# Windowed attention with sinks and a routed block: scores and band masks in 64x64 tiles, casts on GpSimd, weights by the hardware queue

## The chip, the cores and the metric

The kernel runs on one core of a Trainium2 chip. The metric is the device time of one execution in microseconds. A core has five engines with a queue each, worked off in order: TensorE (PE; its weight loads are shown apart as PEld), VectorE (DVE), ScalarE (ACT), GpSimd (POOL) and SyncE (SP), which here only issues DMAs. [...]

## The reference, cut to what matters

B=4 batches, H=8 heads, S=768 positions, D=64. Every query sees the 128 last positions up to its own and the first 4 (the sinks). The result, laid out as rows of 512, goes through a routed block: in each batch the 128 rows with the highest gate score get an update from a two-layer network, scaled by the sigmoid of the score.

```python
scores = scale * np.matmul(q, k.transpose(0, 1, 3, 2))
is_sink = pos[None, :] < 4
in_window = (rel >= 0) & (rel < 128)
a = softmax(np.where(is_sink | in_window, scores, -1e9))
x = np.matmul(a, v)                          # as rows (B, S, H*D)
scores = np.einsum('bsd,d->bs', x, w_gate)
top_idx = the 128 highest of scores[b]
xe = x[b, top_idx]
ye = np.maximum(xe @ w1, 0.0) @ w2           # w1 512x1024, w2 1024x512
out[b, top_idx] = xe + sigmoid(scores)[:, None] * ye
```

## The kernel before

The work is cut into 24 units: 4 batches of 6 blocks of 128 positions. The order on TensorE is written out by hand; the other engines, SP's queue among them, are ordered by a planner that works by program order and its own estimate of when operands are there.

`load_qk` (line 78) issues k and q of one batch on SP in fp32, batch 0 and 1 in 8 pieces of 384 KB, later ones in one piece of 1536 KB each. `load_v` (99) issues the six blocks of v (256 KB, rows of 256 bytes) and, behind the first, eight copies of the four sink rows of a head, 1 KB each, into the packed tile `vsk`. `casts` (92) makes bf16 of a head pair's k on ScalarE and q on VectorE (128x768 each), `transposes` (174) turns them on TensorE into `KT` and `QT` with column tiles of 64, and copies them out on VectorE and ScalarE.

`scores` (198) takes one key block kc and a group g of four heads: four matmuls with 64 rows of contraction (two heads side by side in two row tiles) for 128 keys and 256 queries, the block's own and the next. For kc=0 a matmul of the identity with a mask adds the band to the scores; for other blocks ScalarE takes the exponential (line 218) and GpSimd then sets what lies outside the band to zero with `affine_select` (221, 225). `sink_scores` (229) makes the scores of the four sinks for all queries from position 256 on. `pv_sinks` (237) and `pv` (246) multiply the probabilities, which stand as fp32, with v, which has a column of ones for the sum; an fp32 matmul is two instructions in the trace. VectorE divides (259, 262). `finish_block` (266) stores the block by SP and takes the product with the gate row (269). `compare` (273) spreads the gate scores by a transpose and counts for each row how many lie above it (279). `moe_steps` (285) is cut in five steps that follow in the units of the next batch: the row numbers, an indirect gather by GpSimd (320), a transpose, the two products (336, 342), and an indirect scatter that adds (346).

Per unit u of batch b the loop from line 372 on does: at the first unit of a batch the loads of batch b+1; the scores of the next unit; the sinks of this one; casts of a head pair of batch b+1 (none for the last batch); the values; the sink scores (first unit); the transposes of that head pair; the comparison of the unit before; a step of the routed block of the batch before; the block's store. The network's weights come at unit 1 by two DMAs on GpSimd's queue that cast fp32 to bf16 on the way (line 381), and a dependency makes them wait for the last v of batch 1.

Of the kernel before, what the change touches and what calls it, by code (L numbers as in the profile page):

```python
# [29 lines left out]
def kernel(  # L30
# [17 lines left out]
    qkp = ctx.enter_context(tc.tile_pool(name="qkp", bufs=2))  # L48
# [6 lines left out]
    cmp_p = ctx.enter_context(tc.tile_pool(name="cmp_p", bufs=2))  # L55
# [22 lines left out]
    def load_qk(b, parts):  # L78
        st = BatchState()
        st.b = b  # L80
        st.qf = qkp.tile([128, H, NB, D], FP32, name="qf", tag="qf")
        st.kf = qkp.tile([128, H, NB, D], FP32, name="kf", tag="kf")
        n = H // parts
        for i in range(parts):
            hs = slice(i * n, (i + 1) * n)
            for src, dst in ((k, st.kf), (q, st.qf)):
                nc.sync.dma_start(
                    out=dst[:, hs, :, :].rearrange("p h c d -> p h (c d)"),
                    in_=src[b, hs, :, :].rearrange("h (p c) d -> p h (c d)", c=NB))
        return st  # L90

    def casts(st, hp):
        kb = qbp.tile([128, 2, NB, D], BF16, name="kb", tag="kb")
        qb = qbp.tile([128, 2, NB, D], BF16, name="qb", tag="qb")
        nc.scalar.copy(out=kb[:, :, :, :], in_=st.kf[:, 2 * hp:2 * hp + 2, :, :])  # L95
        nc.vector.tensor_copy(out=qb[:, :, :, :], in_=st.qf[:, 2 * hp:2 * hp + 2, :, :])  # L96
        st.kq[hp] = (kb, qb)

    def load_v(st):
        b = st.b  # L100
        st.v = vbuf[b % 2]
        st.vsk = vsk[b % 2]
        for c in range(NB):
            st.vload = nc.sync.dma_start(
                out=st.v[:, c, :, 0:D],
                in_=v[b, :, c * 128:(c + 1) * 128, :].rearrange("h p d -> p h d"))
            if c == 0:
                for h in range(H):
                    r0 = 32 * (h // 4) + 4 * (h % 4)
                    nc.sync.dma_start(out=st.vsk[r0:r0 + 4, h % 4, 0:D], in_=v[b, h, 0:NSINK, :])  # L110

    st0 = load_qk(0, 4)
    ident_f = cp.tile([128, 128], FP32, name="ident_f", tag="ident_f")
    make_identity(nc, ident_f)


    ident_b = cp.tile([128, 128], BF16, name="ident_b", tag="ident_b")
    nc.vector.tensor_copy(ident_b[:], ident_f[:])  # L118
    for i in range(2):
        nc.vector.memset(vsk[i][:, :, :], 0.0)  # L120
        nc.vector.memset(ksk[i][:, :, :], 0.0)
        nc.vector.memset(vbuf[i][:, :, :, D:D + 1], 1.0)
    load_v(st0)
    ones_f = cp.tile([64, 4], FP32, name="ones_f", tag="ones_f")
    nc.vector.memset(ones_f[:], 1.0)

    for i in range(2):
        for g in range(2):
            o = vsk[i][32 * g:32 * g + 32, :, D:D + 1].rearrange("p h o -> p (h o)")
            nc.gpsimd.affine_select(out=o, in_=ones_f[32 * g:32 * g + 32, 0:4], compare_op=ALU.is_ge,  # L130
                                    fill=0.0, base=0, pattern=[[-4, 4]], channel_multiplier=1)
            nc.gpsimd.affine_select(out=o, in_=o, compare_op=ALU.is_ge,
                                    fill=0.0, base=3, pattern=[[4, 4]], channel_multiplier=-1)

    m0f = cp.tile([128, 256], FP32, name="m0f", tag="m0f")
    nc.vector.memset(m0f[:], 0.0)
    nc.gpsimd.affine_select(out=m0f[:, 0:128], in_=m0f[:, 0:128], compare_op=ALU.is_ge,
                            fill=MASK_NEG, base=0, pattern=[[1, 128]], channel_multiplier=-1)
    nc.gpsimd.affine_select(out=m0f[:, 128:256], in_=m0f[:, 128:256], compare_op=ALU.is_ge,
                            fill=MASK_NEG, base=-1, pattern=[[-1, 128]], channel_multiplier=1)  # L140
    nc.vector.memset(m0f[0:NSINK, :], 0.0)
    mask0 = cp.tile([128, 2, 256], BF16, name="mask0", tag="mask0")
    nc.vector.tensor_copy(out=mask0[:, :, :], in_=m0f[:, :].unsqueeze(1).to_broadcast((128, 2, 256)))

    iota_i = cp.tile([128, 128], mybir.dt.int32, name="iota_i", tag="iota_i")
# [4 lines left out]
    tie = cp.tile([128, S], FP32, name="tie", tag="tie")  # L150
# [5 lines left out]
    beh_i = cp.tile([128, NB], mybir.dt.int32, name="beh_i", tag="beh_i")  # L156
# [5 lines left out]
    rid_i = cp.tile([128, 2, NB], mybir.dt.int32, name="rid_i", tag="rid_i")  # L162
# [8 lines left out]
    w2_sb = wp.tile([128, 8, DM], BF16, name="w2_sb", tag="w2_sb")  # L171


    def transposes(st, hp):
        if hp == 0:
# [15 lines left out]
        for e in range(2):  # L191
            nc.vector.tensor_copy(
                out=st.ksk[64 * e:64 * e + 64, hp, 32 * (hp // 2) + 8 * (hp % 2) + 4 * e:
                           32 * (hp // 2) + 8 * (hp % 2) + 4 * e + 4],
                in_=st.KT[64 * e:64 * e + 64, hp, 0:NSINK])


    def scores(st, kc, g):
# [5 lines left out]
        for hh in range(2):  # L204
            for e in range(2):
                hp = 2 * g + hh
                nc.tensor.matmul(  # L207
                    out=sc[e][:, hh, 0:nq],
                    lhsT=st.KT[64 * e:64 * e + 64, hp, kc * 128:(kc + 1) * 128],
                    rhs=st.QT[64 * e:64 * e + 64, hp, kc * 128:kc * 128 + nq],  # L210
                    start=(hh == 0), stop=(hh == 1 and kc > 0), skip_group_check=True)
        if kc == 0:
            for e in range(2):
                nc.tensor.matmul(out=sc[e][:, :, :], lhsT=ident_b[:, :], rhs=mask0[:, :, :],
                                 start=False, stop=True, skip_group_check=True)
# [3 lines left out]
        if kc > 0:  # L219
            hs = slice(4 * g, 4 * g + 4)  # L220
            nc.gpsimd.affine_select(  # L221
                out=pt[:, hs, 0:128], in_=pt[:, hs, 0:128], compare_op=ALU.is_ge,
                fill=0.0, base=0, pattern=[[0, 4], [1, 128]], channel_multiplier=-1)
            if nq == 256:
                nc.gpsimd.affine_select(  # L225
                    out=pt[:, hs, 128:256], in_=pt[:, hs, 128:256], compare_op=ALU.is_ge,
                    fill=0.0, base=-1, pattern=[[0, 4], [-1, 128]], channel_multiplier=1)

    def sink_scores(st):
        st.psk = sp.tile([64, 512], FP32, name="psk", tag="psk")  # L230
        sk = ps.tile([128, 512], FP32, name="sk", tag="ps")
        for hp in range(HP):
            nc.tensor.matmul(out=sk[:, :], lhsT=st.ksk[:, hp, :], rhs=st.QT[:, hp, 256:S],
                             start=(hp == 0), stop=(hp == HP - 1))
        nc.scalar.activation(out=st.psk[:, :], in_=sk[0:64, :], func=ACT.Exp, scale=0.125)  # L235

    def pv_sinks(st, j):
# [3 lines left out]
        for g in range(2):  # L241
# [205 lines left out]
```

## Time and profile before

| | us |
|---|---|
| median of 3 runs | 184.23 (182.61 to 186.14) |
| the profiled execution | 185.59 |
| its span, first to last instruction | 183.9 |
| TensorE busy | 137.3 (75%) |
| VectorE busy | 108.4 (59%) |
| ScalarE busy | 88.1 (48%) |
| GpSimd busy | 64.3 (35%) |

The profile is one execution. Busy shares are means over stages that differ, so the stretches are read apart. In the order of time an entry merges instructions of one kind that follow each other: its length ends with the last one's end, and matmuls overlap, so the distance between two is the length less one duration, shared by the gaps. The time in brackets is how long the engine stood before the entry, and who released it.

### The profile page before, as it was taken

The numbers are of one execution on the slowest core, as the hardware profiler recorded it, in microseconds if no ns is written. First come the engines' busy times: TensorE is split into PE (matmuls) and PEld (weight loads), VectorE is DVE, ScalarE is ACT, GpSimd is POOL, SyncE is SP. The second block draws the span as 40 slices with busy tenths as digits, with TensorE's granted clock in tenths as the row PEclk, the third lists the DMA queues.
The fourth block names the chain that finished last, engine by engine and source line by source line (L and its number), as shares of the span: only waits on it lengthen the run. The fifth ranks groups of instructions, "written<-read, shape, count | busy, mean of one in ns | idle before, by whom it ended". The sixth has DMA issues, their size and how long they took to land. (4 is left out here: it accounts for less than half of the span.)

```text
span 183.9 us, 5760 instructions
## 1 busy us (share of the span) xinstructions
PE 137.3 (75%) x2418; PEld 98.7 (54%) x2418; DVE 108.4 (59%) x306; ACT 88.1 (48%) x177; POOL 64.3 (35%) x103
## 2 busy tenths in 40 slices
PE   7389978879927209999997499999995889711840
PEld 2154557666806106978664477786574668410710
DVE  5266357998743416477469999782699735740000
ACT  4155677965509206165878085645763533200320
POOL 5100095655154002272009328510596640022020
PEclk9958999999996855699999879999999969965585
DMA  5987999499999987939996941410251311142004
GB/s 178 314 250 152 188 324 368 97 236 298 319 250 264 269 174 153 262 79 286 312 309 119 222 134 61 89 61 4 64 111 57 87 61 61 59 61 29 0 0 57
DMA packets 40074, 29.50 MB, mean 160 GB/s; under 512 B 26096, under 2 KB 35824, under 8 KB 40048
## 3 DMA queue, kind: packets, MB, share of 16 engines
q1 hardware_dynamic: 37328, 25.47, 48.6%
q0 software_dynamic: 2720, 3.67, 12.9%
q8 instruction: 19, 0.31, 0.7%
q14 instruction: 7, 0.06, 0.1%
HBM read 24.41 MB, written 7.34 MB: 173 GB/s over the span
## 5 line engine op out<-in xcount | busy, mean ns | idle before, releaser
L253 PE MATMUL xg<-vbuf,pt 128*64 128x65 f32 x1408 | 51.1, 235 | 3.7 <-DVE x L262 3.7
L253 PEld LDWEIGHTS xg<-vbuf,pt 128*64 128x64 f32 x1408 | 47.5, 148 | 11.9 <-issue 7.9
L221 POOL TENSOR_SCALAR_AFFINE_SELECT pt<-pt 128x512 f32<-128x512 f32 x40 | 32.1, 808 | 57.6 <-ACT pt L218 57.3
L218 ACT ACTIVATE pt<-sc 128x512 f32<-128x512 f32 (+1 forms) x96 | 46.3, 573 | 5.9 <-PE sc L207 3.1
L225 POOL TENSOR_SCALAR_AFFINE_SELECT pt<-pt 128x512 f32<-128x512 f32 x32 | 26.9, 842 | 0.0
L259 DVE RECIPROCAL rz<-xg 128x4 f32<-128x4 f32 x48 | 8.6, 179 | 30.9 <-PE xg L253 30.9
L190 ACT COPY QT<-trp 128x768 bf16<-128x768 bf16 x16 | 12.7, 801 | 27.9 <-PE trp L183 27.9
L207 PE MATMUL sc<-QT,KT 64*128 64x256 bf16 (+1 forms) x192 | 18.0, 272 | 8.3 <-ACT psk L235 4.9
L269 DVE CUSTOM_DVE_ANT_0 junk<-x,wgb 128x512 f32<-128x512 f32 x24 | 21.2, 887 | 0.1
L346 POOL DMA_INDIRECT out_dram<-gye,idx x4 | 6.4, 1608 | 41.8 <-ACT gye L345 32.2
L262 DVE TENSOR_TENSOR x<-xg,rz 128x256 f32<-128x256 f32 x48 | 20.1, 423 | 1.5
L95 ACT CAST kb<-kf 128x768 bf16<-128x768 f32 x16 | 13.1, 848 | 16.6 <-DMA kf<-in_k_dram 10.3
L279 DVE SCALAR_TENSOR_TENSOR cm<-sbc,scol,tie 128x128 bf16<-128x128 f32 (+5 forms) x24 | 18.1, 754 | 4.8 <-ACT sbc L276 4.4
L188 DVE COPY KT<-trp 128x768 bf16<-128x768 bf16 x16 | 15.1, 951 | 4.0 <-PE trp L183 3.7
L96 DVE CAST qb<-qf 128x768 bf16<-128x768 f32 x16 | 10.1, 635 | 11.4 <-DMA qf<-in_q_dram 11.3
L207 PEld LDWEIGHTS <-KT 64*128 64x128 bf16 x192 | 7.5, 95 | 17.1 <-issue 15.2
L183 PE MATMUL trp<-ident_b,qb 128*64 128x128 bf16 x192 | 9.6, 244 | 8.2 <-DVE qb L96 8.2
L276 ACT COPY sbc<-bc 128x128 f32<-128x128 f32 x24 | 6.5, 269 | 15.7 <-PE bc L275 15.7
L242 PE MATMUL xg<-vsk,psk 32*128 32x260 f32 x64 | 12.7, 465 | 0.0
L183 PEld LDWEIGHTS <-qb 128*64 128x64 bf16 x192 | 7.7, 128 | 8.4 <-DVE qb L96 8.4
L183 PE MATMUL trp<-ident_b,kb 128*64 128x128 bf16 x192 | 9.5, 243 | 3.3 <-DVE ident_b L118 3.3
L73 PE MATMUL w<-warm 128*128 128x512 bf16 x30 | 10.7, 514 | 1.3 <-DVE warm L68 1.3
(67 smaller groups left out, 133.2 us busy)
## 6 DMA issues: line engine op xcount, KB each, us to landing
vbuf<-in_v_dram SPq DMA_DIRECT2D x24, 256.0 KB
out_dram<-x SPq DMA_DIRECT2D x24, 256.0 KB
kf<-in_k_dram SPq DMA_DIRECT2D x8, 384.0 KB
qf<-in_q_dram SPq DMA_DIRECT2D x8, 384.0 KB
kf<-in_k_dram SPq DMA_DIRECT2D x2, 1536.0 KB
qf<-in_q_dram SPq DMA_DIRECT2D x2, 1536.0 KB
w_sb<-in_moe_w_dram POOLq DMA_DIRECT2D x2, 1024.0 KB, 18.6
vsk<-in_v_dram SPq DMA_DIRECT2D x32, 1.0 KB
```

The costliest lines, as they stand in the source:

```text
L95: nc.scalar.copy(out=kb[:, :, :, :], in_=st.kf[:, 2 * hp:2 * hp + 2, :, :])
L183: nc.tensor.transpose(out=trp[64 * e:64 * e + 64, c, :], in_=src[:, e, c, :], identity=ident_b[:])
L188: nc.vector.tensor_copy(out=o, in_=i)
L190: nc.scalar.copy(out=o, in_=i)
L207: nc.tensor.matmul(out=sc[e][:, hh, 0:nq], lhsT=st.KT[64 * e:64 * e + 64, hp, kc * 128:(kc + 1) * 128], rhs=st.QT[64 * e:64 * e + 64, hp, ...
L218: nc.scalar.activation(out=po[:, e, :, 0:nq], in_=sc[e][:, :, 0:nq], func=ACT.Exp, scale=0.125)
L221: nc.gpsimd.affine_select(out=pt[:, hs, 0:128], in_=pt[:, hs, 0:128], compare_op=ALU.is_ge, fill=0.0, base=0, pattern=[[0, 4], [1, 128]], ...
L225: nc.gpsimd.affine_select(out=pt[:, hs, 128:256], in_=pt[:, hs, 128:256], compare_op=ALU.is_ge, fill=0.0, base=-1, pattern=[[0, 4], [-1, 1 ...
L253: nc.tensor.matmul(out=xg[64 * m:64 * m + 64, hh, :], lhsT=st.pt[kc][:, h, off + 64 * m:off + 64 * m + 64], rhs=st.v[:, kc, h, :], start=( ...
L262: nc.vector.tensor_tensor(out=st.x[:, 256 * g:256 * g + 256].rearrange("p (h d) -> p h d", h=4), in0=xg[:, :, 0:D], in1=rz[:, :, :].to_bro ...
L269: nc.vector.tensor_tensor_reduce(out=junk[:, :], in0=st.x[:, :], in1=wgb[:, :], scale=1.0, scalar=0.0, op0=ALU.mult, op1=ALU.add, accum_ou ...
L279: nc.vector.scalar_tensor_tensor(out=cm[:, :], in0=st.sbc[:, 0:n], scalar=st.scol[:, j:j + 1], in1=tie[:, S - n:S], op0=ALU.subtract, op1= ...
```

## The change

It makes these edits together. Scores: each 128x128 block of keys becomes two halves, so that score matmuls use 64x64 tiles of the array, and columns that the band never needs are left out. Masks: three 64x64 pieces (`msk`, and `msk0` with the sinks open) are added to the scores by matmuls with a 64x64 piece of the identity, for every key block; the selections on GpSimd go. Sinks: the packed tiles are spread over 128 partitions, sink scores for two head groups stand in two halves of the columns, and the product with the sink values uses 64x64 tiles. The sink rows of v come by two DMAs into `vsr`, and VectorE spreads them into `vsk` with a 0/1 mask. Casts of batch 1 and later are done by GpSimd (as an `affine_select` that selects everything). k and q are kept in half batches of four heads with three buffers. The weights come by SP in four fp32 pieces of 1 MB and are cast by ScalarE. `tie` is bf16, and `cmp_p` has one buffer instead of two.

```diff
 def load_qk(b, parts):
-    (one tile per batch, H // parts heads per DMA)
+    for g in range(2):                       # tiles of 4 heads, bufs=3
+        for i in range(parts):
+            for src, lst in ((k, st.kf), (q, st.qf)):
+                nc.sync.dma_start(out=lst[g][:, n * i:n * i + n, :, :]..., in_=src[b, h0:h0 + n, :, :]...)
 def casts(st, hp):
-    nc.scalar.copy(out=kb[:, :, :, :], in_=st.kf[:, 2 * hp:2 * hp + 2, :, :])
-    nc.vector.tensor_copy(out=qb[:, :, :, :], in_=st.qf[:, 2 * hp:2 * hp + 2, :, :])
+    if st.b == 0:
+        nc.scalar.copy(out=ko, in_=ks)
+        nc.vector.tensor_copy(out=qo, in_=qs)
+    else:
+        for o, i in ((ko, ks), (qo, qs)):
+            nc.gpsimd.affine_select(out=o, in_=i, compare_op=ALU.is_ge, fill=0.0, base=0,
+                                    pattern=[[0, 2 * NB * D]], channel_multiplier=0)
 def load_v(st):
-            if c == 0: for h in range(H): nc.sync.dma_start(out=st.vsk[r0:r0 + 4, h % 4, 0:D], in_=v[b, h, 0:NSINK, :])
+            if c == 1:
+                for R in range(2):
+                    nc.sync.dma_start(out=raw[64 * R:64 * R + 4 * NSINK, :], in_=v[b, 4 * R:4 * R + 4, 0:NSINK, :])
+                nc.vector.tensor_tensor(out=st.vsk[:, :, 0:D], in0=raw..., in1=sel..., op=ALU.mult)
+def load_w(i):
+    wf[i] = ws.tile([128, 2048], FP32, name="wf", tag="wf")          # bufs=3
+    nc.sync.dma_start(out=wf[i]..., in_=src)
+def cast_w(i):
+    src = wf[i // 2][:, 1024 * (i % 2):1024 * (i % 2) + 1024]
+    nc.scalar.copy(out=(w1_sb or w2_sb piece), in_=src)
 def scores(st, kc, g):
-    for hh in range(2): for e in range(2): matmul(sc[e][:, hh, 0:nq], 128 keys, nq queries)
-    if kc == 0: for e in range(2): matmul(sc[e], ident_b, mask0)
+    for hh in range(2):
+        for kh in range(2):
+            q0, q1 = (64, nq) if kh else (0, nq if kc == 0 else min(nq, 192))
+            for e in range(2):
+                nc.tensor.matmul(out=sc[e][es[kh], hh, q0:q1], lhsT=st.KT[es[e], hp, k0:k0 + 64],
+                                 rhs=st.QT[es[e], hp, kc * 128 + q0:kc * 128 + q1], ...)
+    sq = [((2, 4), (0, 2)), ((0, 1), (3, 4))] if nq == 256 else [((0, 1), (0, 2))]
+    for r, pair in enumerate(sq):
+        for kh in range(2):
+            for e in range(2):
+                nc.tensor.matmul(out=sc[e][es[kh], :, 64 * s0:64 * s1]..., lhsT=ident_b[es[e], es[e]],
+                                 rhs=m[es[e], :, m0:m0 + s1 - s0, :], ...)
-    if kc > 0: (affine_select of columns 0:128, and of 128:256)
 def sink_scores(st):
-    for hp in range(HP): matmul(sk[:, :], ksk 128 columns, QT[:, hp, 256:S])
+    for hp in (0, 2, 1, 3): matmul(sk[es[hp // 2], :], ksk 64 columns, QT[:, hp, 256:S])
 def pv_sinks(st, j):
-    for g in range(2): matmul(xg[g][:, :, :], psk[32 * g:32 * g + 32, 128 queries], vsk[32 * g:32 * g + 32])
+    for m in range(2):
+        for g in range(2):
+            nc.tensor.matmul(out=st.xg[g][es[m], :, :], lhsT=st.psk[es[g], q0:q0 + 64], rhs=st.vsk[es[g], :, :], ...)
 # the loop
-            if u == 1: (two gpsimd.dma_start of w1, w2 behind the last v of batch 1)
+                if b == 0:
+                    for i in range(3): load_w(i)          # behind load_v of batch 1
...
             for hp in hps:
                 transposes(states[b + 1], hp)
+            if b == 1 and j < 4:
+                cast_w(2 * j)
+                cast_w(2 * j + 1)
+                if j == 0:
+                    load_w(3)
```

## Rows read from the trace of the kernel before

**Rows 1.** The page: engine totals, then 40 slices of the span (DMA in tenths, GB/s moved).

```profile
PE 137.3 (75%) x2418; PEld 98.7 (54%) x2418; DVE 108.4 (59%) x306; ACT 88.1 (48%) x177; POOL 64.3 (35%) x103
...
DMA  5987999499999987939996941410251311142004
GB/s 178 314 250 152 188 324 368 97 236 298 319 250 264 269 174 153 262 79 286 312 309 119 222 134 61 89 61 4 64 111 57 87 61 61 59 61 29 0 0 57
```

**Rows 2.** Busy us by stretch: length, each engine's busy time (instructions), granted clock, DMA share, GB/s.

```profile
21.10:50.90 29.80, 26.39 (x570) 19.63 (x570) 22.92 (x66) 21.69 (x44) 15.30 (x22) 1.00 0.96 267
50.90:77.30 26.40, 13.28 (x214) 10.75 (x212) 10.53 (x31) 8.81 (x17) 6.99 (x11) 0.68 1.03 227
...
99.90:107.00 7.10, 3.35 (x69) 3.09 (x68) 6.93 (x15) 1.67 (x4) 2.68 (x5) 0.81 1.03 230
...
136.00:153.00 17.00, 13.06 (x259) 10.31 (x260) 12.15 (x34) 6.57 (x17) 9.93 (x15) 0.90 0.19 56
...
157.50:184.00 26.50, 10.14 (x85) 6.63 (x81) 5.09 (x16) 3.74 (x8) 4.17 (x3) 0.65 0.21 36
```

**Rows 3.** TensorE in order of time: start us, length us, instructions [wait before, released by].

```profile
56.54 0.58 PE L207 MATMUL sc<-QT,KT 64*128 64x256 bf16 x3 [4.92 <-ACT psk L235]
...
68.96 0.85 PE L183 MATMUL trp<-ident_b,qb 128*64 128x128 bf16 x12 [8.20 <-DVE qb L96]
...
72.66 3.73 PE L253 MATMUL xg<-vbuf,pt 128*64 128x65 f32 x64
...
103.68 1.53 PE L253 MATMUL xg<-vbuf,pt 128*64 128x65 f32 x32 [3.75 <-DVE x L262]
...
141.51 0.29 PE L275 MATMUL bc<-ident_f,scol 128*128 128x128 f32 x1 [1.62 <-DVE scol L269]
```

**Rows 4.** ScalarE and VectorE in order of time, around those waits.

```profile
55.17 0.83 ACT L95 CAST kb<-kf 128x768 bf16<-128x768 f32 x1 [4.18 <-DMA kf<-in_k_dram]
...
68.35 0.56 DVE L96 CAST qb<-qf 128x768 bf16<-128x768 f32 x1 [5.75 <-DMA qf<-in_q_dram]
...
97.64 4.97 DVE L304 SCALAR_TENSOR_TENSOR rid<-scol,rid 128x6 bf16<-128x6 f32 x1
...
138.02 3.34 DVE L269 CUSTOM_DVE_ANT_0 junk<-x,wgb 128x512 f32<-128x512 f32 x1
```

**Rows 5.** SP and GpSimd in order of time: DMA issues.

```profile
7.21 7.04 SPq L110 DMA_DIRECT2D vsk<-in_v_dram  x8
...
49.33 0.60 SPq L87 DMA_DIRECT2D qf<-in_q_dram  x1
...
44.10 1.93 POOL L381 DMA_DIRECT2D w_sb<-in_moe_w_dram  x2 [2.27 <-DMA vbuf<-in_v_dram]
```

**Rows 6.** TensorE in one steady unit, and groups by shape: count, busy us, mean ns.

```profile
110.94 0.51 PE L183 MATMUL trp<-ident_b,kb 128*64 128x128 bf16 x12
...
131.48 1.04 PE L233 MATMUL sk<-QT,ksk 128*128 128x512 bf16 x4
...
136.63 0.61 PE L207 MATMUL sc<-QT,KT 64*128 64x256 bf16 x8
137.17 0.71 PE L242 MATMUL xg<-vsk,psk 32*128 32x260 f32 x4
137.81 2.09 PE L253 MATMUL xg<-vbuf,pt 128*64 128x65 f32 x64
...
L207 PE MATMUL sc<-QT,KT 64*128 64x256 bf16 x160 | 15.8, 282 | 6.7 <-ACT psk L235 4.9 <-DVE KT L188 1.4
...
L183 PE MATMUL trp<-ident_b,kb 128*64 128x128 bf16 x192 | 9.5, 243 | 3.3 <-DVE ident_b L118 3.3
...
L233 PE MATMUL sk<-QT,ksk 128*128 128x512 bf16 x16 | 4.1, 382 | 0.0
```

**Rows 7.** GpSimd groups by shape: count, busy us, mean ns of one.

```profile
L221 POOL TENSOR_SCALAR_AFFINE_SELECT pt<-pt 128x512 f32<-128x512 f32 x40 | 32.1, 808 | 57.6 <-ACT pt L218 57.3
...
L139 POOL TENSOR_SCALAR_AFFINE_SELECT m0f<-m0f 128x128 f32<-128x128 f32 x1 | 0.3, 293 | 0.1
```

More of the change, by code (lines that the diff above doesn't have):

```diff
@@ L80, in load_qk @@
         st.b = b
[L81 to L89, printed above, removed]
+        st.kq = {}
+        st.qf, st.kf = [], []
+        n = 4 // parts
+        for g in range(2):
+            for lst, nm in ((st.kf, "kf"), (st.qf, "qf")):
+                lst.append(qkp.tile([128, 4, NB, D], FP32, name=nm, tag=nm))
+            for i in range(parts):
+                for src, lst in ((k, st.kf), (q, st.qf)):
+                    h0 = 4 * g + n * i
+                    nc.sync.dma_start(
+                        out=lst[g][:, n * i:n * i + n, :, :].rearrange("p h c d -> p h (c d)"),
+                        in_=src[b, h0:h0 + n, :, :].rearrange("h (p c) d -> p h (c d)", c=NB))
         return st
@@ L119 @@
     for i in range(2):
-        nc.vector.memset(vsk[i][:, :, :], 0.0)
+        nc.vector.memset(vsr[i][:, :], 0.0)
         nc.vector.memset(ksk[i][:, :, :], 0.0)
         nc.vector.memset(vbuf[i][:, :, :, D:D + 1], 1.0)
-    load_v(st0)
[L124 to L133, printed above, removed]
@@ L218, in scores @@
             nc.scalar.activation(out=po[:, e, :, 0:nq], in_=sc[e][:, :, 0:nq], func=ACT.Exp, scale=0.125)
[L219 to L227, printed above, removed]
     def sink_scores(st):
-        st.psk = sp.tile([64, 512], FP32, name="psk", tag="psk")
+        st.psk = sp.tile([128, 512], FP32, name="psk", tag="psk")
         sk = ps.tile([128, 512], FP32, name="sk", tag="ps")
[L232 to L235, printed above, removed]
+        for hp in (0, 2, 1, 3):
+            nc.tensor.matmul(out=sk[es[hp // 2], :], lhsT=st.ksk[:, hp, :], rhs=st.QT[:, hp, 256:S],
+                             start=(hp % 2 == 0), stop=(hp % 2 == 1), skip_group_check=True)
+        nc.scalar.activation(out=st.psk[:, :], in_=sk[:, :], func=ACT.Exp, scale=0.125)
     def pv_sinks(st, j):
@@ L240, in pv_sinks @@
             return
[L241 to L244 removed]
+        for m in range(2):
+            for g in range(2):
+                q0 = (j - 2) * 128 + 64 * m
+                nc.tensor.matmul(out=st.xg[g][es[m], :, :], lhsT=st.psk[es[g], q0:q0 + 64],
+                                 rhs=st.vsk[es[g], :, :], start=True, stop=False, skip_group_check=True)
     def pv(st, j, g):
```

134 lines of the change are left out of this document (81 added, 53 removed).

## The prediction

> **What bounds the kernel now.** I read the page's totals and slices first, then the busy time by stretches, then TensorE's own order of time with the waits in it, and last the engines named as releasers. TensorE is busy 75% of the span and no other engine over 59% [rows 1]. But that share is an average over unlike stretches. From 21.1 to 50.9 us TensorE is busy 26.4 of 29.8 us at full clock; from 50.9 to 77.3 us it is busy half the time, at a granted clock of 0.68; in 99.9 to 107 and 136 to 153 it loses time again; the last 26.5 us are the chain of the last gather, two products and scatter [rows 2]. So the kernel is a TensorE pipeline of some 5 us per unit with four holes and a tail. The DMA slices stand mostly at seven tenths or more through the first 22 (of 4.6 us each) and at half or far less in the last third [rows 1]: the first 70 us are also a transfer problem.
>
> The holes: 4.92 us before the scores at 56.54, put down to ScalarE's sink exponential, and 8.20 us before the transposes at 68.96, put down to VectorE's q cast [rows 3]. Neither engine was slow: ScalarE stood 4.18 us in front of a cast waiting for k of batch 2, VectorE 5.75 us for its q [rows 4]. Both queues are in order, so everything behind stood too. [...] The other holes have another cause: at 103.68 TensorE waited 3.75 us for VectorE, where a 128x6 operation took 4.97 us while GpSimd worked off a backlog of mask selections; at 141.51 it waited 1.62 us for a gate product that took 3.34 us beside GpSimd [rows 3, 4].
>
> Why q of batch 2 is late: SP spends 7.04 us on issuing eight 1 KB sink rows in batch 0 (the same again in batch 1), so k and q of batch 1 and 2 are issued late; at 44.10 GpSimd's two weight transfers start, released by the last v of batch 1, and share the DMA engines with k and q (issued at 49.33) [rows 5].
>
> **The change part by part**, against the profiled execution's own 185.59 us (span 183.9 plus 1.7 outside it), which is 1.4 us over the median of the runs shown.
>
> *Scores and masks.* Today 192 score matmuls and 16 mask matmuls; after: per head pair half and key block 8 scores in 64x64 tiles of 192 or 256 columns and 8 masks of 256 or 128 columns (4 for the last key block), 736 in all. Rows for the pace: 8 scores in two row tiles take 0.61 us, 0.28 of it the last one's own duration, so 47 ns apart; a 512-column matmul on the whole array 0.22 us ((1.04-0.38)/3), so 0.43 ns a column, and 256 columns alone would be 110 ns: the row tiles overlap. Transposes in column tiles (64 columns of weights each, 128 streamed) stand 24 ns apart ((0.51-0.244)/11), the value matmuls at most 33 (2.09/64) [rows 6]. No row shows 64x64 tiles. Lower bound: four tiles overlap, 192 columns cost 20 ns of streaming and the pair is held by the 24 ns seen. Middle: only two overlap, 16x41+8x55+8x28 = 1.32 us per 32 pairs, 41 ns each. Upper: none overlap, 82 ns each. I take 24 ns, the row it is nearest to (own weights of 64 columns, another tile each time): 736 x 24 = 17.7 us against 160x47+32x28+16x220 = 11.9 us today: +5.8 us (two-way +18; none +48). The exponentials read the same tiles in the same time.
>
> [...]
>
> *Sinks.* The scores pass into the sinks with a change of tile today: 0.54 us from the first score to the first sink, 8x47 = 0.38 of it at pace, so 0.16 us; after, both are 64x64 and it goes. The 4 instructions (0.64 us) become 8 in four tiles, the same streaming. 16 units: -2.6 us. The sink scores become two column tiles at once, four times 4 x 0.22 us to half of it: -1.7 us [rows 6]. So TensorE's own work changes by +1.5 us.
>
> *GpSimd.* 72 selections of 0.81 us, 58 us, go. 24 casts come: 512 elements 808 ns, 128 elements 293 ns, so 768 elements 1.15 us, 28 us in all [rows 7]; below, 0.81, what 512 elements take; above, twice 1.15, since writing bf16 is shown nowhere. Two casts one after the other replace two side by side (0.83 and 0.56 us [rows 4]), +1.5 us from arrival to transposes, hidden where q and k come a unit ahead. With the masks gone from GpSimd nothing long is left beside VectorE in batch 3 and little in batch 2: the hole at 99.9 (3.75 us and about 1.2 of lower clock) I count at -4.5; the 3.34 us gate product and what its lateness does to the gather (1.62 us [rows 3], and a clock of 0.90 over 17 us, 1.7 us [rows 2]) at -3. In batch 0 the q casts leave a VectorE busy 22.9 of 29.8 us [rows 2]: -1.
>
> *Transfers.* Eight sink issues become two: at 0.88 us each SP gains 5.3 us a batch, 10 us before k of batch 2. Weights come as 1 MB pieces by SP: three right behind v of batch 1, the fourth behind v of batch 2. Every piece is an issue of SP and stands before the output rows. Until the first half of k and q of batch 2: 2 x 4.72 + 0.26 + 3.15 + 1.57 (six outputs) + 1.57 = 16.0 MB. The kernel now has the first 9.7 MB landed by 44.1 us; without the two 5.3 us that is about 36. The other 6.3 MB take 24 us at the 267 GB/s of that stretch [rows 2], or 17 at the 368 of the best slice [rows 1]: 53 to 60 us. With two casts 55 to 62. TensorE reaches these transposes at 60.3 us today (8.20 before 68.96, less the 0.5 of the k ones [rows 3]); without its 4.92 us and 1.3 of lower clock it wants them at 54. A wait of 1 to 8 us is left; I take 4.5, and 1.5 for the clock. Today the stretch pays 13.1 us of waits; its 13.28 busy us at a mean clock of 0.68 hold 13.28 x 0.32 = 4.3 us of lower clock [rows 2]: -11.4 us.
>
> *ScalarE.* 12 casts of 0.83 us go, 8 weight casts of 1024 elements come, 1.11 us by length: two per unit in the first four of batch 1. ScalarE is busy 21.7 of 29.8 us in batch 0 [rows 2], 3.6 us in a unit of 5; with 2.2 in the place of one 0.83 us cast that is 5.0, as much as the unit has. Scores run a unit ahead, so I count +1.5. Behind a waiting weight cast stand the exponentials and the q copies, and TensorE behind these: if a piece lands late the hole comes back. The same holds for VectorE, which now multiplies the packed sinks by a mask as soon as its plan says they have landed.
>
> Sum: -11.4 -4.5 -3 -1 +1.5 +1.5 = -16.9; 185.6 - 16.9 = 168.7; less the 1.4 by which the profile stands above the median: 167.
>
> **The rivals.**
> *The wait moves* (0.16). q of batch 2 lands at 65 or the in-order queues of ScalarE and VectorE stand before the weights or the packed sinks: 8 to 11 of the 11.4 us stay, 176 to 180 us, a few over. For it: the planner already put the k cast in front of the sink exponential 4 us too early [rows 4], and the bytes are the same. Against it: the SP time that goes is certain.
> *Pairs no faster than today's scores* (0.09). Each 64x64 pair holds TensorE 47 ns [rows 6]: 736 x 23 = +17, 184 us, no change. For it: every pair carries a weight load, and the scores too have one each. Against it: transposes at 24.
> *64x64 tiles don't overlap* (0.10), the slower case: 82 ns a pair, 736 x 58 = +43, 210 us. It decides above 50 ns a pair; between 50 and 82 the time is 188 to 210. For it: no row has the two kinds of tile at once. Against it: each kind alone overlaps.
> *No wait is left* (0.10): q lands by 52, ScalarE keeps up: 167 - 6 - 1.5 - 3 = 156 us.
>
> **How the numbers follow.** Likeliest is the sum, 167, its own range 160 to 176 (0.55). 156 to 184 leaves out the slower case, and little below. A measurement of this kernel tells about 2% from no change, that is 180.5 to 188. Faster: 0.55 + 0.10 + 0.13 of the moved wait = 0.78; same: 0.09 + 0.03 = 0.12; slower 0.10.
>
> **What would show it.** Right: no wait over 5 us before the first transposes of batch 2; the granted clock at its upper level from there to the tail; score and mask pairs 24 to 30 ns apart; no VectorE operation of over 2 us; SP at the gate row and k of batch 1 some 5 us sooner; the tail unchanged at 26 us. Wrong: pairs over 45 ns; ScalarE idle in front of a weight cast, or VectorE in front of the packed sinks, with TensorE idle behind it; GpSimd casts of over 2 us. What would overturn it: a changed order at the start (the bf16 identity, on VectorE behind two q casts, sets the first transposes), which the trace can't tell.

## The result, and the profile after

| | us |
|---|---|
| before, median of 4 runs beside the changed kernel | 185.19 (182.61 to 188.62) |
| after, median of 4 runs | 173.15 (171.97 to 175.05) |
| ratio after to before | 0.942, 95% interval 0.923 to 0.960 |
| the profiled execution of after, its span | 175.05, 173.3 |

The changed kernel is faster by 12 us of median: inside the range that was forecast, 6 us short of the sum. Some executions of one kernel come out 1.5% or more above its fastest; the ratios here leave these out, the medians don't. The profiled execution is the longest of the four; the same kernel was profiled once more later (`c2_after_again`, median 172.71 us, span 169.3), and what is said of one profile below is held against the other.

The page of after, with the lines that answer to [rows 1] (totals; 40 slices, here of 4.3 us; the queues):

```profile
PE 129.0 (74%) x3010; PEld 99.4 (57%) x3010; DVE 96.8 (56%) x303; ACT 87.4 (50%) x173; POOL 35.1 (20%) x51
...
PEclk9999999999755999996599999999999999955585
DMA  5999999899999799999869971311161411142004
GB/s 178 296 338 200 148 333 371 180 222 313 297 377 333 219 345 185 168 348 379 299 211 229 209 213 61 46 60 64 64 121 64 99 61 66 61 61 30 0 0 61
...
q8 instruction: 23, 0.38, 0.9%
```

GpSimd's busy time falls from 64.3 to 35.1 us, VectorE's by 11.6, TensorE's by 8 though it has 592 matmuls more (3010 against 2418). But TensorE's share of the span is what it was. The granted clock, a share of full speed, has two dips ahead of the tail, in the eleventh to thirteenth and the nineteenth and twentieth slice: it is 0.50 in 45.6 to 55.5 us and in 80 to 86.2, and 1.00 in 56 to 79 between them. The stretches of after show them (length, each engine's busy time and instructions, clock, DMA share, GB/s; compare [rows 2]):

```profile
21.10:43.00 21.90, 17.34 (x508) 14.19 (x507) 14.35 (x40) 11.63 (x25) 7.18 (x8) 1.00 1.01 279
43.00:57.00 14.00, 6.77 (x121) 4.82 (x118) 3.79 (x13) 8.49 (x13) 1.18 (x2) 0.63 0.97 337
57.00:75.50 18.50, 15.98 (x471) 13.25 (x459) 17.00 (x49) 11.15 (x25) 7.15 (x8) 1.00 0.96 240
75.50:87.00 11.50, 6.75 (x126) 5.66 (x126) 3.46 (x12) 4.52 (x9) 2.77 (x4) 0.70 0.95 325
87.00:113.00 26.00, 24.64 (x653) 20.10 (x655) 20.26 (x60) 17.39 (x36) 6.88 (x7) 1.00 0.68 167
113.00:146.50 33.50, 31.86 (x859) 26.34 (x850) 21.68 (x75) 19.20 (x45) 2.79 (x2) 1.00 0.26 73
146.50:173.50 27.00, 10.22 (x91) 6.69 (x85) 5.09 (x17) 3.75 (x8) 4.16 (x3) 0.65 0.22 34
```

From 87 us to the tail at 146.5 TensorE is busy 95% of the time at full clock (1.00): the holes of [rows 3] at 103.68 and 141.51 have no successors. But in 43 to 57 it is busy less than half, where the kernel before was busy for 9.08 of the same 14 us, at a clock of 0.98, and again in 75.5 to 87. So the lost time of batch 1 has moved to other places. TensorE in order of time names them:

```profile
27.02 0.27 PE L268 MATMUL sc<-msk,ident_b 64*64 64x256 bf16 x4 [1.49 <-issue]
...
33.59 0.30 PE L268 MATMUL sc<-msk,ident_b 64*64 64x256 bf16 x4 [1.72 <-issue]
...
45.14 0.27 PE L257 MATMUL sc<-QT,KT 64*64 64x192 bf16 x2 [1.99 <-issue]
...
52.27 1.14 PE L291 MATMUL xg<-vsk,psk 64*64 64x260 f32 x6 [5.24 <-DVE x L310]
...
62.28 0.51 PE L227 MATMUL trp<-ident_b,kb 128*64 128x128 bf16 x12
...
80.29 0.61 PE L375 MATMUL xeT<-ident_b,xe 128*128 128x128 bf16 x4 [4.75 <-DMA xe<-out_dram,idx]
...
82.48 3.73 PE L301 MATMUL xg<-vbuf,pt 128*64 128x65 f32 x64
```

The first transposes of batch 2, at 62.28, no longer wait: the 8.20 us at 68.96 are gone. In their place stand 5.24 us for VectorE's output rows, 4.75 us for the routed block's gather, each with matmuls at the lower clock behind it (the 64 value matmuls of a unit take 3.73 us at 82.48, where the clock is 0.50, and 2.09 at 119.59, where it is 1.00), and three waits, 5.2 us together, with no releaser at all ("issue": the profile shows nothing that TensorE waited for). VectorE was not slow at 52: it stood itself, for a store to land and free one of the four buffers of a block's rows:

```profile
51.79 0.76 DVE L310 TENSOR_TENSOR x<-xg,rz 128x256 f32<-128x256 f32 x2 [7.40 <-DMA out_dram<-x]
```

SP in order of time shows what stood before that store; the chain of work, taken from 36 to 85 us, how long that store, and later the gather, then took:

```profile
36.39 2.84 SPq L207 DMA_DIRECT2D wf<-in_moe_w_dram  x3
39.33 2.30 SPq L315 DMA_DIRECT2D out_dram<-x  x4
41.72 0.96 SPq L93 DMA_DIRECT2D kf<-in_k_dram  x1
52.57 0.33 SPq L315 DMA_DIRECT2D out_dram<-x  x1
52.95 0.43 SPq L93 DMA_DIRECT2D qf<-in_q_dram  x1
```

```profile
39.33 12.44 DMA out_dram<-x
...
71.61 8.63 DMA xe<-out_dram,idx
```

Three weight pieces of 1 MB are issued just ahead of four finished blocks of output. 3.15 MB at the 337 GB/s of 43 to 57 us would be 9.3 us (an estimate), and the store takes 12.44 where the page's median is 5.3. Until it lands, at 51.77 us, VectorE can't write the fifth block, and SP, in order, holds the next store and q of batch 2 behind it, to 52.95; the kernel before issued that q at 49.33 [rows 5]. The gather of 71.61 lands 8.63 us later, where the page's median is 3.8, while the queues move 294 GB/s (71.61 to 80.24 us): four stores, v of batch 2, the fourth weight piece and k and q of batch 3 are under way with it.

The starts of the value matmuls cut every kernel's span into the same five parts: up to the values of unit (0,1), the second of batch 0; from there to the first values of batch 2; from there to the first of batch 3; from there to the values of the last unit; the rest (us, one profile each):

```
                      start   to batch 2   batch 2   batch 3   rest    span
before                24.6      71.1        34.7      25.1     28.4    183.9
after                 22.0      73.1        29.3      20.3     28.6    173.3
c2_after_again        23.8      69.2        28.2      19.9     28.2    169.3
a1_six_x              24.1      66.1        29.5      20.4     27.8    167.7
a2_w_behind_q         24.1      60.6        33.5      20.0     28.6    166.8
a3_both               23.8      63.6        32.2      20.1     28.9    168.7
a4_w_gpsimd           23.2      65.7        29.4      20.2     27.8    166.3
b1_masks_only         21.5      74.2        30.9      21.1     28.9    176.5
b2_casts_back         24.8      68.4        29.6      19.7     28.6    171.1
b4_sinks_in_pieces    23.7      70.6        30.0      19.8     28.9    173.1
b3_no_masks           22.5      69.1        28.6      20.3     28.7    169.2
c1_shifted            22.1      69.9        29.0      19.8     28.8    169.6
```

After gains 5.4 and 4.8 us in batches 2 and 3, and next to nothing before them (0.6 us; 2.7 in c2).

### The profile page after: what moved, and what is told of

It is laid out like the page before. It is cut to its first block, busy times and chain, and to the rows that moved or that the text cites. A ratio compares the mean times of both kernels' runs of the same rounds, so it can differ in the third digit from the quotient of the medians.

```text
span 173.3 us, 6858 instructions
## 1 busy us (share of the span) xinstructions
PE 129.0 (74%) x3010; PEld 99.4 (57%) x3010; DVE 96.8 (56%) x303; ACT 87.4 (50%) x173; POOL 35.1 (20%) x51
## 4 chain that ended last, share of the span: by engine, by line
PE 35%; DMA 24%; DVE 13%; SPq 12%; issue 9%; ACT 2%; POOLq 1%
PE xg L301 16%; DMA xe<-out_dram,idx 9%; DMA qf<-in_q_dram 8%; DMA out_dram<-x 7%; SPq L120 6%; PE xg L291 3%; PE sc L257 3%; PE hps L385 3%; PE ye L391 3%; DVE x L310 3%; DVE KT L232 3%; SPq L126 2%; DVE cm L328 2%; SPq L207 2%; PE sc L268 2%
## 5 line engine op out<-in xcount | busy, mean ns | idle before, releaser
L274 ACT ACTIVATE pt<-sc 128x512 f32<-128x512 f32 (+1 forms) x96 | 46.8, 578 | 10.6 <-PE sc L268 10.5
L257 PE MATMUL sc<-QT,KT 64*64 64x192 bf16 (+3 forms) x384 | 19.3, 250 | 6.6 <-DVE KT L232 3.4
L111 POOL TENSOR_SCALAR_AFFINE_SELECT kb<-kf 128x768 bf16<-128x768 f32 x12 | 10.2, 865 | 63.6 <-DMA kf<-in_k_dram 37.9
L268 PE MATMUL sc<-msk,ident_b 64*64 64x256 bf16 (+1 forms) x352 | 17.3, 248 | 3.2 <-issue 3.2
L317 DVE CUSTOM_DVE_ANT_0 junk<-x,wgb 128x512 f32<-128x512 f32 x24 | 17.4, 726 | 2.3 <-DMA wgb<-in_moe_w_gate_dram 2.2
L257 PEld LDWEIGHTS <-KT 64*64 64x64 bf16 x384 | 9.5, 107 | 12.6 <-issue 10.0
L291 PE MATMUL xg<-vsk,psk 64*64 64x260 f32 x128 | 12.6, 416 | 5.2 <-DVE x L310 5.2
L268 PEld LDWEIGHTS <-ident_b 64*64 64x64 bf16 x352 | 10.8, 109 | 3.7 <-issue 3.7
L111 POOL TENSOR_SCALAR_AFFINE_SELECT qb<-qf 128x768 bf16<-128x768 f32 x12 | 10.8, 915 | 6.1 <-PE xg L301 3.3
L227 PEld LDWEIGHTS <-kb 128*64 128x64 bf16 x192 | 6.8, 113 | 5.6 <-issue 5.0
L385 PE MATMUL hps<-xeT_sb,w_sb 128*128 128x128 bf16 x128 | 9.4, 242 | 0.7 <-ACT xeT_sb L377 0.7
```

The costliest lines, as they stand in the source:

```text
L111: nc.gpsimd.affine_select(out=o, in_=i, compare_op=ALU.is_ge, fill=0.0, base=0, pattern=[[0, 2 * NB * D]], channel_multiplier=0)
L227: nc.tensor.transpose(out=trp[64 * e:64 * e + 64, c, :], in_=src[:, e, c, :], identity=ident_b[:])
L257: nc.tensor.matmul(out=sc[e][es[kh], hh, q0:q1], lhsT=st.KT[es[e], hp, k0:k0 + 64], rhs=st.QT[es[e], hp, kc * 128 + q0:kc * 128 + q1], sta ...
L268: nc.tensor.matmul(out=sc[e][es[kh], :, 64 * s0:64 * s1].rearrange("p h (s n) -> p h s n", n=64), lhsT=ident_b[es[e], es[e]], rhs=m[es[e], ...
L274: nc.scalar.activation(out=po[:, e, :, 0:nq], in_=sc[e][:, :, 0:nq], func=ACT.Exp, scale=0.125)
L291: nc.tensor.matmul(out=st.xg[g][es[m], :, :], lhsT=st.psk[es[g], q0:q0 + 64], rhs=st.vsk[es[g], :, :], start=True, stop=False, skip_group_ ...
```

## The experiments

**The theory and its rivals.** Theory: the edits of masks and casts gave what batches 2 and 3 gained, and the k and q holes did go; but the weights, put on SP ahead of the output rows, made new waits that took that gain back. Rivals: the waits are the x buffers alone; the load on the queues alone, whoever issues it; the new tiles themselves.

**More buffers for the rows.** `a1_six_x`:

```diff
-    xp = ctx.enter_context(tc.tile_pool(name="xp", bufs=4))
+    xp = ctx.enter_context(tc.tile_pool(name="xp", bufs=6))
+    junk = cp.tile([128, DM], FP32, name="junk", tag="junk")
-        junk = sp.tile([128, DM], FP32, name="junk", tag="junk")
```

> The changed kernel with six buffers for the output rows instead of four (the scratch of the gate product gets one buffer to make room). Theory 1, buffers: VectorE stood 7.40 us because the rows of unit 4 need the buffer of unit 0, whose store lay behind three weight pieces; with six the 5.24 us wait of TensorE and the lower clock behind it (1.07 to 3.16 us entries) go, 7 us, of which 2 to 3 come back as a wait for q of batch 2: 167 to 169 us. Theory 2, bytes: the DMA engines are full until 57 us anyway, so q of batch 2 lands when it did and the wait only changes its name: 171 to 174 us.

Measured: 171.58 us, ratio 0.933 (0.917 to 0.950), which can't be told from after's 0.942. The wait of line 310 is gone. SP shows what came in its place (line numbers one up):

```profile
38.96 11.22 SPq L316 DMA_DIRECT2D out_dram<-x  x6
50.27 0.39 SPq L94 DMA_DIRECT2D kf<-in_k_dram  x1
```

Six blocks of output now stand in one row before k of batch 2, which is issued at 50.27 instead of 41.72. One wait went; the queue behind the weights stayed as long.

**The weights behind k and q.** `a2_w_behind_q` keeps four row buffers and issues the first three pieces at the start of batch 1, behind k and q of batch 2 and ahead of its v; their casts and the fourth piece come one unit later:

```diff
                 states[b + 1] = load_qk(b + 1, 2 if b == 0 else 1)
-                load_v(states[b + 1])
-                if b == 0:
+                if b == 1:
                     for i in range(3):
                         load_w(i)
+                load_v(states[b + 1])
...
-            if b == 1 and j < 4:
+            if b == 1 and 1 <= j < 5:
```

> The changed kernel with the first three weight pieces issued behind k and q of batch 2 (and in front of its v), the fourth one unit later, the weight casts one unit later. Four x buffers as in the changed kernel. Theory 1: the stores of units 0 to 3 now stand in front of the weights, VectorE does not wait for a buffer, k and q land by 50 us: 165 to 168 us. Theory 2: weights then delay v of batch 2 and the gather of batch 0, whose wait grows from 4.75 to 8 us: 170 to 174 us.

Measured: 167.29 us, ratio 0.899 (0.884 to 0.913), which lies wholly below after's. SP in order of time:

```profile
35.57 4.93 SPq L315 DMA_DIRECT2D out_dram<-x  x4
40.60 0.39 SPq L93 DMA_DIRECT2D kf<-in_k_dram  x1
...
47.15 0.43 SPq L93 DMA_DIRECT2D qf<-in_q_dram  x1
...
51.39 1.80 SPq L207 DMA_DIRECT2D wf<-in_moe_w_dram  x3
```

With the same four buffers no wait for them is left: the stores go out at 35.57 and land in time, and q is issued 5.8 us sooner than in after. The first gather lands within 4.6 us, where the queues move 202 GB/s (65 to 69.6 us), and TensorE doesn't wait for it. The stretch up to batch 2 shrinks to 60.6 us, 10.5 less than before. Some of it is given back in batch 2 (33.5 us, 29.3 in after), in part by a wait without a releaser and a clock of 0.72 behind it (93 to 99 us):

```profile
93.37 0.25 PE L227 MATMUL trp<-ident_b,kb 128*64 128x128 bf16 x2 [2.49 <-issue]
```

Such waits did not go with the weights: in after's list of waits they add up to 5.5 us, in a2's to 8.9. The gain of a2 came in spite of them.

**Both.** `a3_both` is a1's and a2's edits together.

> Six x buffers and the weights behind k and q of batch 2 together. Theory 1: as the better of the two alone, 164 to 168 us, since either one takes the same wait away. Theory 2: 170 to 174 us.

Measured: 166.99 us, ratio 0.906 (0.897 to 0.916), no different from a2. Once the weights are out of the way two more buffers are worth nothing that can be measured: the order of the queue had made them short.

**The weights by GpSimd.** `a4_w_gpsimd` undoes that part of the change: the casting DMAs of the kernel before, on GpSimd's queue, released by the last v of batch 1. ScalarE casts no weights.

```diff
-                if b == 0:
-                    for i in range(3):
-                        load_w(i)
+            if u == 1:
+                for wi, src in ((w1_sb, moe_w1...), (w2_sb, moe_w2...)):
+                    ins = nc.gpsimd.dma_start(out=wi[:], in_=src)
```

> The changed kernel with the weights as in the kernel before: two casting DMAs on GpSimd's queue behind the last v of batch 1, no weight casts on ScalarE. By the prediction the weights by hardware queue were part of what brings q of batch 2 in time: with this undone the wait before the first transposes of batch 2 is over 5 us and the time 174 to 178 us. By the reading of the changed trace (weights in front of the stores cost 5.24 us and the clock) nothing is lost by undoing it: 169 to 174 us.

Measured: 168.75 us (166.62 to 171.4), against 186.35 of the kernel before beside it; no interval can be given for these few runs. The first reading, over 5 us before the first transposes of batch 2, fails: they wait 1.3 us for the cast of q, which lands at 58.6 us, no sooner than in after. The weights start at 41.15 us, so they load the DMA engines in the same stretch as after's do (1.10 of their time in 43 to 57 us, at 243 GB/s); but SP issues the four stores at 36.63 and q at 47.13, and TensorE waits for no rows: it is busy 12.1 of these 14 us, 6.77 in after. That speaks for the place in SP's order, and against load alone, as what cost some 4 us; the load was not the same, 243 GB/s against 337. The change's way with weights was a loss where it was put, and between a2 and a4, 1.5 us apart, the measurement can't choose.

**The masks alone.** `b1_masks_only` is the kernel before with `scores` in 64x64 tiles and the masks on TensorE (no `affine_select` on the probabilities); casts, values, sinks and weights are those of before.

> The kernel before with one part of the change alone: scores and band masks in 64x64 tiles, so that GpSimd clears no triangles; casts, values, sinks and weights are those of before. Theory: the hole of 4.5 us at 99.9 and the 3 us of batch 3 were GpSimd's triangles beside VectorE, and go with them, while the waits of the first pairs of batch 2 for k and q stay: 8 us under the kernel before, some 177 us, and VectorE's longest operation falls from 4.97 us to under 2. Rival, that those holes went because the casts left VectorE and ScalarE: no more than 2 us under the kernel before, with a long operation of VectorE still there. Second rival, that the pairs of tiles cost more than they save while the casts stay where they were: 2 us or more over it.

Measured: 179.56 us against 186.38, ratio 0.971 (0.954 to 0.987): some 5 us by the ratio, 6.8 by the medians. In the table batches 2 and 3 give 3.8 and 4.0; what lies before batch 2 ends at 95.7 us in both. Its longest operation on VectorE is 1.08 us, where there were 4.97 and 3.34 [rows 4]; the group that it belongs to (count, busy us, mean ns):

```profile
L287 DVE SCALAR_TENSOR_TENSOR cm<-sbc,scol,tie 128x768 bf16<-128x768 f32 x4 | 4.1, 1032 | 3.8 <-ACT sbc L284 3.8
```

The holes of batches 2 and 3 go with this part of the change alone, then, as they should if GpSimd's selections made them. The first pairs of batch 2 still wait, 6.7 us for q in b1's list of waits:

```profile
PE trp L189 <- DVE qb L96: 6.7, 1, 6.7
```

**The casts back.** `b2_casts_back`: `if st.b == 0:` in `casts` becomes `if True:`, so all casts are ScalarE's and VectorE's.

> The changed kernel with the casts of batches 1 to 3 on ScalarE and VectorE again, as batch 0's are. Theory: with the triangles gone, what the move of the casts to GpSimd brings is the busy time of VectorE and ScalarE (some 8 casts of 0.8 us on each, in stretches in which TensorE decides): within 3 us of the changed kernel, 171 to 176 us. Rival, that VectorE and ScalarE wait in order behind casts whose k or q is late, as in the kernel before, and hold up the units behind them: 5 us or more over the changed kernel, with a wait of over 3 us at line 107 or 108 at 43 to 60 us.

Measured: 174.75 us, ratio 0.948 (0.934 to 0.962); after had 0.942 and, as c2, 0.957 (0.939 to 0.975). No difference that can be told. The in-order rival falls too: none of the casts at lines 107 and 108 between 43 and 60 us waits for its k or q, and the longest such wait later is 2.08 us.

**The sinks in pieces.** `b4_sinks_in_pieces` brings the sinks of v in eight 1 KB copies a batch again, into the new places, without the product on VectorE.

> The changed kernel with the sinks of v brought by eight copies of 1 KB a batch straight to their places, in place of two copies and a multiplication by VectorE. Theory: SP issues six copies more a batch, some 4 us of its time, ahead of k and q of the next batch and of output rows, and VectorE has 0.7 us less a batch: 0 to 4 us over the changed kernel. Rival, that SP's time costs nothing since the transfers behind it are late for the queues anyway: within 1 us, or up to 2 us under it.

Measured: 174.93 us against 186.38; no interval can be given for these few runs. SP spends 8.64 us on the eight of batch 0 where after spends 3.15 on two, and q of batch 2 is issued at 57.08 instead of 52.95; TensorE waits 10.4 us for rows, twice after's wait. So SP's time was not free. Yet the time is only some 2 us over after's two medians, which 4 runs hardly tell from nothing: the waits without a releaser, 5.5 us in after's list, are 0.6 us here. These need the next two runs.

**Fewer instructions.** Each of the three waits stands in a stretch in which queue 8 has one of its packets of 16 KB (24.7 to 27.2, 30 to 34 and 42 to 46 us; the other queues take 1.05, 0.84 and 0.96 of the DMA engines' time there). There are 23 such packets in all and 6020 instructions of matmul and weight load, 262 to a packet, and 19 for 4836 before, 255 to a packet. `b3_no_masks` leaves out the masks of key blocks 1 to 5 (their scores take all columns), so its outputs lack the band there:

```diff
-                q0, q1 = (64, nq) if kh else (0, nq if kc == 0 else min(nq, 192))
+                q0, q1 = (0, nq) if kc else (64, nq) if kh else (0, nq)
-        for r, pair in enumerate(sq):
+        for r, pair in enumerate(sq if kc == 0 else []):
```

> The changed kernel with fewer instructions of TensorE: the band masks of all units but the first of a batch are left out, and their scores take the whole stretch of columns (this leaves out a part of the computation). Theory: TensorE's idle times of 1.5 to 2 us with no releaser, which stand where a queue of 16,384-byte packets has a packet under full load of the hardware queues, are the fetching of its own instructions: with some 270 matmuls fewer of 3010 that queue has 2 or 3 packets fewer and one or two of these waits go or move to other instructions: 2 to 4 us under the changed kernel, of which the masks' own time is some 270 at 22 ns in pairs, 3 us at most. Rival, that they come from the tiles themselves (a switch between tile shapes): the waits that are left stand at the same instructions, and where the queues are quiet too.

Measured: 171.29 us, ratio 0.925 (0.912 to 0.938); 21 packets. One long wait is left, and it stands in the value matmuls:

```profile
34.42 0.62 PE L301 MATMUL xg<-vbuf,pt 128*64 128x65 f32 x14 [1.88 <-issue]
```

The place moved away from the small tiles. The time moved by about 1%, and with it the wait for rows (7.1 us, 5.24 in after): nothing can be read from the time itself.

**Shifted by 64.** `c1_shifted` adds 64 matmuls of zeros at the start, where TensorE has no data yet, and nothing else:

```diff
         keep_warm(14)
+        for _ in range(64):
+            nc.tensor.matmul(out=w2[:, 0:64], lhsT=warm[:, 0:128], rhs=warm[:, 0:64], start=True, stop=True)
```

> The changed kernel with 64 small matmuls (64 columns of zeros) more at the start, where TensorE waits for its first data; nothing else. Theory: TensorE's waits without a releaser are the fetching of its instructions in blocks; 64 matmuls with their 64 weight loads are half a block, so the waits come 64 matmuls earlier in the order of work: those which stood inside the band masks and scores of the units at 27.0, 33.6 and 45.1 us stand inside the matmuls of line 301 of the unit before, up to 2 us each, and the number of instruction packets stays at 23 or goes to 24. Rival, that they come from the change of tile shapes (or from the masks themselves): they stay inside lines 257 and 268 of the same units.

Measured: 171.33 us in one run, 24 packets. TensorE in order of time:

```profile
25.89 1.73 PE L301 MATMUL xg<-vbuf,pt 128*64 128x65 f32 x51
29.77 0.62 PE L301 MATMUL xg<-vbuf,pt 128*64 128x65 f32 x13 [2.15 <-issue]
...
63.98 0.24 PE L268 MATMUL sc<-msk,ident_b 64*64 64x128 bf16 x2 [1.75 <-issue]
```

After's second wait stood some 25 instructions into the scores and masks of unit (0,3). Back from there come one spreading matmul and 24 transposes, so 64 matmuls earlier is some 50 into the 64 values of unit (0,2); the wait stands after 51. The first and third are not found in their new places, and a new one of 1.75 us stands in a mask at 63.98. A count explains all of these. Busy time by stretch, from the start to just before c1's two waits (the first number in brackets counts TensorE's matmuls, the second its weight loads):

```profile
0.00:29.76 29.76, 25.00 (x478) 16.11 (x478) 14.88 (x56) 16.41 (x27) 7.76 (x25) 1.00 0.96 275
0.00:63.97 63.97, 51.84 (x1114) 37.45 (x1115) 37.50 (x120) 36.84 (x65) 16.88 (x35) 0.92 0.97 287
```

The same for a2, up to a wait of 1.33 us among its value matmuls, and that wait:

```profile
0.00:62.11 62.11, 50.33 (x1114) 36.54 (x1115) 40.45 (x124) 34.22 (x63) 16.59 (x35) 0.92 0.92 274
```

```profile
62.12 0.97 PE L301 MATMUL xg<-vbuf,pt 128*64 128x65 f32 x26 [1.33 <-issue]
```

After's three waits have 350, 477 and 732 matmuls ahead of them. In the nine runs that have such waits (after, a1 to a4, b2, b3, c1, c2) all that last 0.3 us or more come after 350, 477 (478 in c1), 732, 860, 987 (986 in b3), 1114, 1242, 1497, 1624 or 1751 matmuls, that is 127 or 128 or twice as many apart, and 127 matmuls with their weight loads are 254 instructions, about one packet by the 255 and 262 above; one wait alone (0.88 us in a2, after 1193) doesn't fit. The instruction that stands there differs: the 477 are followed by masks in after and by values in b3 and c1, the 1114 by values in a2 and by a mask in c1. So the place goes with the count of instructions and not with the tile.

Whether a place costs time is another matter, and this stays open. In after the first and third wait fell into stretches in which the queues moved 392 and 372 GB/s, the second into one of 191 (30 to 34 us); in b4, with TensorE's instructions those of after, the second place cost 0.40 us, at 35.46, in a stretch of 98 GB/s (34 to 40 us). That suggests that the packets come late where the queues are full, but it is not shown: the kernel before and b1 have no such wait at all, with 19 and 23 packets, four of them in 21.1 to 50.9 us, where the queues moved 267 and 258 GB/s. What the record does show is that the three kernels with eight sink copies a batch (before, b1, b4) lose 0 to 0.6 us by these waits, and the nine with two copies 2.7 to 8.9; a run that moves the load and nothing else was not made.

**The changed kernel again.** `c2_after_again` is after, unaltered.

> The changed kernel once more, unaltered, beside it. Every theory: 172 to 175 us; waits without a releaser of 1 to 2 us inside lines 257 and 268 near 27, 34 and 45 us, a wait of line 291 for x buffers of some 5 us near 52 us, and one of some 5 us for the gather near 80 us, if the first profile was typical of it. If one of them is missing at the same time as before, it was an accident of that execution and not a cost of the change.

Measured: 172.71 us, ratio 0.957 (0.939 to 0.975). The waits of its TensorE in order of time:

```profile
28.11 0.27 PE L268 MATMUL sc<-msk,ident_b 64*64 64x256 bf16 x4 [1.27 <-issue]
...
34.67 0.43 PE L268 MATMUL sc<-msk,ident_b 64*64 64x256 bf16 x4 [1.72 <-issue]
...
46.79 0.27 PE L257 MATMUL sc<-QT,KT 64*64 64x192 bf16 x2 [1.11 <-issue]
...
51.58 1.14 PE L291 MATMUL xg<-vsk,psk 64*64 64x260 f32 x6 [3.62 <-DVE x L310]
...
79.15 0.61 PE L375 MATMUL xeT<-ident_b,xe 128*128 128x128 bf16 x4 [3.58 <-DMA xe<-out_dram,idx]
```

All five stand at the same instructions as in after, each as long or shorter; the part up to batch 2 is 4 us shorter. They belong to the kernel; their size varies.

## Why the prediction was right, and where its sum was not

Forecast 167, faster, range 156 to 184; measured 173.15. The sign and the likeliest case's own range (160 to 176) hold. Of the terms one failed, and one thing was not in the sum at all; larger gains elsewhere covered part of both.

*Transfers, -11.4: failed.* The holes it names did go, all 13.1 us of waits and 4.3 of lower clock, and k and q came when the working said: their first casts on GpSimd run from 55.82 to 60.18 us (forecast: done at 55 to 62), and the transposes behind them don't wait:

```profile
55.82 1.61 POOL L111 TENSOR_SCALAR_AFFINE_SELECT kb<-kf 128x768 bf16<-128x768 f32 x2 [21.68 <-DMA kf<-in_k_dram]
58.40 1.78 POOL L111 TENSOR_SCALAR_AFFINE_SELECT qb<-qf 128x768 bf16<-128x768 f32 x2 [0.97 <-DMA qf<-in_q_dram]
```

But what the term left was 6 us, and what came was 5.24 + 4.75 + 5.2 us of waits and 6.77 x 0.37 + 6.75 x 0.30 = 4.5 us of lower clock, 19.7 in all against 17.4 that went. The working counted bytes up to k and q and asked only when these land. Its sentence "Every piece is an issue of SP and stands before the output rows" had no price behind it: which engine waits for those rows was not asked, and it was VectorE, for their buffers. The sign that the clock would stand at its upper level (1.00) from the first transposes of batch 2 to the tail failed with it: it was 0.70 in 75.5 to 87 us, behind the gather. With the weights elsewhere the term is there: in a2 batch 2 begins 10.95 us sooner than before (24.1 + 60.6 against 24.6 + 71.1), though 4 us of that come back in batch 2 itself, and the whole kernel takes 167.3 us.

The 5.2 us of waits without a releaser are not the weights' doing: a2 and a4, with the weights elsewhere, have 8.9 and 7.0 us of them. The sum had nothing for what 592 more matmuls ask of the instruction queue, and no trace of the kernel before could have shown it, as it has no such wait.

The rival "the wait moves" is what happened, and within its price for the term, 8 to 11 us; but it was looked for at ScalarE, behind the weight casts, and at VectorE, before the packed sinks, and it stood at the rows' buffers. The gains of batches 2 and 3, larger than forecast, kept the time under that rival's 176. That the time lies in the likeliest case's range is therefore luck: its main term came out as the rival had it.

*GpSimd: -4.5, -3 and -1.* Right as a mechanism, and b1 shows it by itself (no VectorE operation over 1.08 us without the selections, 4.97 and 3.34 with them). Batches 2 and 3 gave 5.4 and 4.8 us (6.5 and 5.2 in c2), 10.2 together where 7.5 were forecast, of which the masks alone make 7.8; the rest is not told apart. The casts cost 0.87 and 0.92 us against 1.15, and in b2 they were worth nothing measurable, either way. Groups of after by shape (count, busy us, mean ns; compare [rows 7] for the casts, [rows 6] for the rest):

```profile
L257 PE MATMUL sc<-QT,KT 64*64 64x192 bf16 x288 | 16.4, 251 | 5.4 <-DVE KT L232 2.9 <-issue 2.0 <-ACT pt L274 0.3
L268 PE MATMUL sc<-msk,ident_b 64*64 64x256 bf16 x176 | 15.4, 276 | 3.2 <-issue 3.2
...
L111 POOL TENSOR_SCALAR_AFFINE_SELECT qb<-qf 128x768 bf16<-128x768 f32 x12 | 10.8, 915 | 6.1 <-PE xg L301 3.3 <-DMA qf<-in_q_dram 2.6
...
L111 POOL TENSOR_SCALAR_AFFINE_SELECT kb<-kf 128x768 bf16<-128x768 f32 x12 | 10.2, 865 | 63.6 <-DMA kf<-in_k_dram 37.9 <-PE bc L324 20.7 <-PE trp L227 4.7
...
L215 ACT CAST w_sb<-wf 128x1024 bf16<-128x1024 f32 x4 | 4.0, 1056 | 1.0 <-DMA wf<-in_moe_w_dram 1.0
```

*Scores and masks, 24 ns a pair: right.* TensorE in order of time, a group of scores and masks:

```profile
24.74 0.36 PE L257 MATMUL sc<-QT,KT 64*64 64x192 bf16 x8
24.93 0.34 PE L268 MATMUL sc<-msk,ident_b 64*64 64x256 bf16 x8
25.09 0.34 PE L257 MATMUL sc<-QT,KT 64*64 64x192 bf16 x8
```

Sixteen start within 25.09 - 24.74 = 0.35 us: 22 ns each, though one alone shows 251 or 276 ns, and 192 columns would stream for 82 ns at the 0.43 ns a column that the prediction took from [rows 6]. So about four are at work at once (an estimate, 82/22 = 3.7), and both rivals on the pairs (47 and 82 ns) fall. TensorE's own work stayed level: two units of batch 2 stand 5.1 us apart before and after.

*Sinks and SP.* Four sink scores take 0.60 us instead of 1.04, as forecast. The two sink copies cost SP 3.15 us, not the 1.76 the working took, so SP gains 3.9 us a batch. b4, which gives this back, has k and q of batch 2 some 4 us later (their first casts at 59.93 and 62.52 us, 55.82 and 58.40 in after) and is some 2 us slower; how much of the 4 us its fewer waits without a releaser hide isn't told apart.

*ScalarE, +1.5: nothing.* The weight casts took 1.06 us each (1.11 forecast); six of them lay in the hole at 46 to 53 us and two in that at 77 to 79, so what they would cost without these holes isn't shown. TensorE's list of waits has none for ScalarE over 0.7 us. What follows from the last unit's values on, some 28.5 us, is unchanged, as said.

## What to carry to other kernels

When a change puts transfers on a queue, price them for everything that stands behind them there, above all for stores whose buffers an engine needs back, and not only for the load that they were meant to help: here 3 MB of weights whose first product came at 87 us stood in front of 1 MB of stores whose buffers were needed at 47, and cost some 4 us against the old way. A hole that a trace shows may be only the first to end in a stretch that the transfers fill; ask what is late next, and try the order of issues before more buffers. Small tiles, started 22 ns apart, took mask work off GpSimd here, and TensorE's time for a unit stayed at 5.1 us. But 592 matmuls more came with 4 packets more on the instruction queue: look for waits without a releaser at even steps of the count.

## What the runs showed of the hardware

Not expected were the waits of TensorE with no releaser, up to 2.5 us each, at fixed counts of its instructions, 127 or 128 matmuls with their weight loads, or a multiple, apart: 592 matmuls more came with 4 packets more on the instruction queue (23 against 19), and in after, c2 and a1 to a4 these places cost 4.1 to 8.9 us of the whole, in the kernel before and in b1 nothing. And a 64x64 bf16 matmul of 192 or 256 columns with its own weights, four tiles in turn, was issued every 22 ns (sixteen of them in 0.35 us, from 24.74 us in after).
